# Skewing the two head halves of the output product in a recurrent attention kernel

## The chip, the cores and the metric

The kernel runs on one core of a Trainium2 chip. The core has a matrix engine (TensorE, PE in the profile; its weight loads are shown as PEld), VectorE (DVE), ScalarE (ACT), GpSimd (POOL), and SyncE (SP), which issues most of the DMAs. Each engine works through its own queue of instructions, and the engines wait for each other by semaphores.

The metric is the device time of one execution in microseconds (us); less is better. Where a kernel was run several times, the median is given.

## What is computed

Two sublayers on a sequence of 2048 tokens with 640 features. The first is attention that runs segment by segment: each segment of 32 tokens is put behind 8 memory tokens, and the attention output at those 8 places is the memory of the next segment. So the 64 segments form a chain. The second is a feed-forward layer with a squared ReLU, which has no such chain. Cut to what matters here:

```python
for s in range(n_seg):                                # 64 segments of 32 tokens
    xs = x[:, s * seg_len:(s + 1) * seg_len, :]
    h = jnp.concatenate([mem, xs], axis=1)            # 8 memory rows + 32 tokens
    q = jnp.einsum('btd,dhe->bhte', h, Wq)            # 32 heads of 128
    k = jnp.einsum('btd,dhe->bhte', h, Wk)
    v = jnp.einsum('btd,dhe->bhte', h, Wv)
    scores = jnp.einsum('bhqe,bhke->bhqk', q, k) * scale
    p = _softmax(jnp.where(mask[None, None], scores, -1e9), axis=-1)
    o = jnp.einsum('bhqk,bhke->bhqe', p, v)
    o = jnp.einsum('bhte,hed->btd', o, Wo)            # the output product
    mem = o[:, :M, :]                                 # carried to the next segment
    outs.append(o[:, M:, :])
...
h = x + attention(layernorm(x))
h2 = h + relu(layernorm(h) @ w1 + b1) ** 2 @ w2 + b2
```

## The kernel before, in words

**Strips.** The matrix array is used in four column strips of 32: a matmul with 32 columns of weights is written to rows 32k to 32k+31 of a PSUM tile, where k is the strip, and matmuls of different strips can run side by side. A projection (`proj`, L194) runs over five chunks c of the 640 features; for each chunk it issues four matmuls of 512 columns, one for each strip.

**Steps.** `step(b, sp)` (L368) is one segment; b counts blocks of 128 tokens and sp the four segments in one. It projects q and k (L450 to L470) for 32 rows (8 memory rows and the first 24 tokens of the segment), then v, with the scores (L401, L478), the softmax of the memory rows and their values (L431) put in between. What the memory rows do not need is deferred: the token rows' softmax (L523 to L538) runs on DVE, ACT and POOL beside the output product, and the tokens' values are formed one step later (`token_values`, L336). The last eight tokens of each segment ("tails") depend on no memory of their own segment's chain for their projections, so these are made ahead, for four segments at a time.

**Fill.** Work that can be done at any time is kept in a list `fill` of units; `run(fill, n)` (L249) calls the next n. A unit is one chunk of a tail projection (`tail_units`, L257: four matmuls of 512 columns, ten units for one tensor and block) or one tenth of a tail output product (`wo_tail_units`, L285: one or two rounds of four matmuls of 320 columns). The loop at L715 adds ten units to most steps; some steps get five, a few none. A step calls one unit at L509, two at L520, five at L549 between the output product and `mem_to_hT`, and the rest at L553. The last unit of a projected half evacuates its PSUM tile with ScalarE (`tail_out`, L272).

**The output product and what hangs on it.** `wo_rounds` (L229) sums over 32 heads in 16 rounds. Each round has four matmuls of 320 columns: strips 0 and 1 (`kh` = 0) hold the two halves of the 640 features for one half of the heads, strips 2 and 3 (`kh` = 1) the same for the other half of the heads. `wo_out` (L239) then adds the two head halves: ScalarE copies rows 64 to 127 of the PSUM tile `pw` to `otmp` (L243), and VectorE adds them to rows 0 to 63 (L244) to give `o`. From `o`, `mem_to_hT` (L304) makes the transposed memory rows by 20 small matmuls (L308) and a VectorE cast into `hT4` (L310). The first projection of the next step reads `hT4`.

Two other readers stand near. `token_out` (L351) lets ScalarE write the previous segment's token outputs into `oT`, the tile that the output product reads (L353), and then POOL copies the tails' share (L355); `tails_in` (L312) lets POOL place the tail rows of q and k (L314, L315). `store_main` (L328) has SP store `o`.

**Order and waits.** The program is in manual order: every engine gets its instructions in the order in which this code emits them. The waits between engines are put in by the framework, from the tiles that each instruction reads and writes.

Of the kernel before, what the change touches and what calls it, by code (L numbers as in the profile page):

```python
# [11 lines left out]
F32 = mybir.dt.float32  # L12
# [4 lines left out]
def kernel(  # L17
# [16 lines left out]
    nc = tc.nc  # L34
    _, S, D = A_x.shape
    _, H, E = A_Wq.shape
# [6 lines left out]
    DC = D // 128  # L43
    DH = D // 2
# [23 lines left out]
    s1 = ctx.enter_context(tc.tile_pool(name="s1", bufs=1))  # L68
# [31 lines left out]
    oT = const.tile([128, H, NK], BF16)  # L100
    nc.vector.memset(oT[:], 0.0)
    oTts = [const.tile([128, H, 32], BF16, name="oTt%d" % k) for k in range(2)]
# [3 lines left out]
    def head(p):  # L106

        n, g, j = p // 16, p // 4 % 4, p % 4
        return g * HG + j * 2 + n
# [25 lines left out]
    for ch in range(2):  # L135
        nc.sync.dma_start(out=o0[32 * ch:32 * ch + M, :].rearrange("m (c f) -> m c f", f=64),
                            in_=A_mem0[0].rearrange("m (c t f) -> t m c f", t=2, f=64)[ch])
# [53 lines left out]
            hT4s[b] = hT4  # L191
        return out

    def proj(w, by, lhs, n, ps, c0, c1):  # L194

        if by == "columns":
            wr = w[:].rearrange("p (c g j n k e) -> p c n k g j e", c=DC, g=G, n=2, j=4, k=4)
        elif by == "half":
            wr = w[:].rearrange("p (c k j n e) -> p c n k j e", c=DC, k=G, n=2, j=4)
        else:  # L200
            wr = w[:].rearrange("p (c k n f) -> p c n k f", c=DC, k=G, n=2)
        for c in range(c0, c1):
            for k in range(4):
                nc.tensor.matmul(ps[32 * k:32 * k + 32, :], lhsT=lhs(c), rhs=wr[:, c, n, k], start=(c == 0), stop=(c == DC - 1))  # L204

    def mmtile():
        return mm.tile([128, 512], F32, tag="mm", name="ps")
# [18 lines left out]

    wov2 = wo[:].rearrange("p h (c t f) -> p h t c f", t=2, f=64)

    def wo_rounds(lhs, pw, h0, h1):  # L229

        for h in range(h0, h1):
            for kh in range(2):
                for ch in range(2):
                    j = kh * 2 + ch
                    p = h // 8 * 16 + kh * 8 + h % 8
                    nc.tensor.matmul(pw[32 * j:32 * j + 32, 0:DH], lhsT=lhs(p), rhs=wov2[:, head(p), ch],  # L236
                                     start=(h == 0), stop=(h == 15))

    def wo_out(pw):  # L239
        o = o_ring[0]  # L240
        o_ring.append(o_ring.pop(0))
        tmp = s1.tile([128, DH], F32, tag="tk", name="otmp")
        nc.scalar.copy(out=tmp[0:64], in_=pw[64:128, 0:DH])  # L243
        nc.vector.tensor_tensor(out=o[0:64], in0=pw[0:64, 0:DH], in1=tmp[0:64], op=ALU.add)  # L244
        return o

    fill, late, mid, win = [], [], [], []

    def run(q, n):  # L249
        while n > 0 and q:  # L250
            q.pop(0)()
            n -= 1

    def tail_rows(b, c):
        return hTts[b // 4][:, c, b % 4].rearrange("p k s -> p (k s)")

    def tail_units(b, which):  # L257
        w = {"q": wq, "k": wk, "v": wv}[which]
        lhs = lambda c: tail_rows(b, c)
        st = {}  # L260

        def unit(n, c):
            def f():
                if c == 0:
                    st[n] = mmtile()
                proj(w, "columns" if which != "v" else "order", lhs, n, st[n], c, c + 1)
                if c == DC - 1:
                    tail_out(b, which, n, st[n][:])
            return f
        return [unit(n, c) for n in range(2) for c in range(DC)]  # L270

    def tail_out(b, which, n, ps):  # L272
        row = parked.pop(0) if which == "v" and 0 < b and parked else rowtile()[:]
        evac_row(which, row, ps)
        if which == "v":
            eng = nc.sync if b else nc.scalar
            eng.dma_start(out=vt_d[b, 2 * n:2 * n + 2].rearrange("j r f -> r j f"),
                          in_=row.rearrange("r (j f) -> r j f", j=2))
            return
        if n == 0:  # L280
            tails.setdefault(b, {})[which] = s2.tile([128, H, 32], BF16, tag=which + "Tt", name=which + "Tt")
        dst = tails[b][which]
        late.append(lambda: flip(row, dst, n))

    def wo_tail_units(b):  # L285
        st = {}

        def out():
            o = wo_out(st["ps"])
            dst = o_all[:].rearrange("(b s t) d -> b s t d", s=4, t=SEG)  # L290
            for ch in range(2):
                nc.sync.dma_start(out=dst[b, :, HD:SEG, ch * DH:(ch + 1) * DH], in_=o[32 * ch:32 * ch + 32, :])

        def unit(k):
            def f():
                if k == 0:
                    st["ps"] = mmtile()
                wo_rounds(lambda p: oTts[b % 2][:, p, :], st["ps"], k * 16 // 10, (k + 1) * 16 // 10)
                if k == 9:
                    late.append(out)  # L300
            return f
        return [unit(k) for k in range(10)]

    def mem_to_hT(o, hT4, sp):  # L304
        pm = chn.tile([128, 512], F32, tag="ch", name="pm")
        for c in range(DC):
            for q in range(4):
                nc.tensor.matmul(pm[32 * q:32 * q + 32, c * M:(c + 1) * M], lhsT=o[:, (2 * c + q % 2) * 32:(2 * c + q % 2 + 1) * 32],  # L308
                                 rhs=ident[:, q // 2 * 32:q // 2 * 32 + M], start=True, stop=True)
        nc.vector.tensor_copy(out=hT4[:, :, sp, 0:M], in_=pm[:, 0:DC * M].rearrange("p (c m) -> p c m", m=M))  # L310

    def tails_in(b, sp):  # L312
        q, k = [tails[b][w][:].rearrange("p h (k s) -> p h s k", s=4)[:, :, sp, :] for w in "qk"]
        nc.gpsimd.tensor_copy(out=qT[:, :, SEG:NK], in_=q)  # L314
        nc.gpsimd.tensor_copy(out=kT[:, :, SEG:2 * SEG].rearrange("p h (j k) -> p h j k", k=TL),  # L315
                              in_=k.unsqueeze(2).to_broadcast([128, H, 4, TL]))
# [51 lines left out]
    def step(b, sp, v=None):  # L368
# [3 lines left out]
        lhs = lambda c: hT4[:, c, sp, :]  # L372
        ready = v is not None
        if not ready:
            v = s2.tile([128, EG], BF16, tag="v", name="v")
# [4 lines left out]
        def project(which, w, dst, n, between=None):  # L380
            if ready:
                if between:
                    between()
                return
            ps = mmtile()
            proj(w, "columns", lhs, n, ps, 0, DC)
            row = rowtile()
            if not between:
                evac_row(which, row[:], ps[:])
                flip(row[:], dst, n)  # L390
                return
            for u in range(2):
                nc.scalar.copy(out=row[:, u * 256:(u + 1) * 256], in_=ps[:, u * 256:(u + 1) * 256])  # L393
            between()
            for u in range(2):
                nc.vector.transpose(out=dst[:, n * 16 + u * 8:n * 16 + u * 8 + 8, 0:32],
                                    in_=row[:, u * 256:(u + 1) * 256].rearrange("p (h e) -> p h e", e=32))
# [74 lines left out]
        if not ready:  # L472
            ps0 = mmtile()
            proj(wv, "half", lhs, 0, ps0, 0, 2)
# [49 lines left out]
        tk = s1.tile([128, HG, NK], F32, tag="tk", name="tk")  # L524
# [14 lines left out]
                                op=ALU.mult)  # L539

        pw = chn.tile([128, 512], F32, tag="ch", name="pw")
        wo_rounds(lambda p: oT[:, p, 0:32], pw, 0, 16)
        o = wo_out(pw)
        if s:
            token_out(s - 1, po)
        if s > 1:
            store_main(o, s - 2)
        if not last:
            run(fill, 5)  # L549
            mem_to_hT(o, hT4s[(s + 1) // 4], (s + 1) % 4)  # L550
            tails_in((s + 1) // 4, (s + 1) % 4)
        run(mid, 2)
# [162 lines left out]
    for b in range(NB):  # L715
        for sp in range(4):
# [39 lines left out]
            if 2 <= e <= NK4 + 1:  # L756
                late.append(lambda e=e: prep_stats0(e - 2))
                mid.append(lambda e=e: prep_norm0(e - 2))
            step(b, sp, v0 if b + sp == 0 else None)

    def end_output(s):
        pw = chn.tile([128, 512], F32, tag="ch", name="pw")
        wo_rounds(lambda p: oT[:, p, 0:32], pw, 0, 16)
        store_main(wo_out(pw), s)
# [15 lines left out]
    for t in range(S // NT):  # L780
        hnT = hnTs[t % 2]
        more = t + 1 < S // NT
        got, hts, mvs, hn_ = {}, {}, {}, {}
# [3 lines left out]
        for fc in range(FC):  # L787
            ps = mmtile()
# [8 lines left out]
            w = NT if fc < FFULL else HT  # L797
# [3 lines left out]
            if more and fc >= 1 and (fc - 1) // 3 < NK4:  # L801
                k, stage = divmod(fc - 1, 3)
# [10 lines left out]
        for q in range(NK4):  # L813
# [6 lines left out]
            for hh in range(2):  # L820
                k = pr + 2 * hh
# [3 lines left out]
                if more and q and (hh == 0 or q == 1):  # L825
                    k = q if hh == 0 and q > 1 else hh
# [5 lines left out]
            for hh in range(2):  # L832
                b = t * NK4 + pr + 2 * hh
# [38 lines left out]
```

## Time and profile before

| What | Value |
|---|---|
| Time, median of 3 runs | 1039.55 us (1038.3 to 1039.93) |
| Span of the profiled execution | 1035.5 us |
| TensorE busy in it | 980.1 us (95%) |
| First output product of the chain | at 66.10 us |
| 64 output products (L236 into pw), to | 906 us |
| L236 matmuls into pw | x4224, 159.6 us busy |
| Mean of one matmul of 320 columns | 300 ns |
| Mean of one matmul of 512 columns (L204) | 379 ns |
| Copy L243, mean of one | 422 ns |
| Add L244, mean of one | 482 ns |

The span runs from the first to the last instruction of the profiled execution; the time of a run has some 4 us more around it. A busy time is the union over an engine's instructions: four matmuls of 300 ns that run side by side count little more than one. In the page's groups the columns are line, engine, operation, output and inputs by name, count, then busy time and the mean of one, then the idle time of the engine just before and what ended it. In a timeline a bracket gives the idle time of that engine before the group and the instruction that ended it.

### The profile page before, as it was taken

The numbers are of one execution on the slowest core, as the hardware profiler recorded it, in microseconds if no ns is written. First come the engines' busy times: TensorE is split into PE (matmuls) and PEld (weight loads), VectorE is DVE, ScalarE is ACT, GpSimd is POOL, SyncE is SP. The second block draws the span as 40 slices with busy tenths as digits, with TensorE's granted clock in tenths as the row PEclk, the third lists the DMA queues.
The fourth block names the chain that finished last, engine by engine and source line by source line (L and its number), as shares of the span: only waits on it lengthen the run. The fifth ranks groups of instructions, "written<-read, shape, count | busy, mean of one in ns | idle before, by whom it ended". The sixth has DMA issues, their size and how long they took to land.

```text
span 1035.5 us, 58905 instructions
## 1 busy us (share of the span) xinstructions
PE 980.1 (95%) x26960; PEld 563.9 (54%) x26960; DVE 621.6 (60%) x1740; ACT 536.0 (52%) x1225; POOL 312.3 (30%) x805
## 2 busy tenths in 40 slices
PE   5879899999999999999999999999999998999998
PEld 2335455555655555555555655555555555555565
DVE  2155666766566666666666666666666676565432
ACT  2435555555555555555555555555555555534431
POOL 1033333333333333332333233333333333343210
PEclk9889999999999999999999999999999999999999
DMA  8960101000100000000000000000000110612200
GB/s 319 405 205 26 22 7 31 7 24 6 32 10 22 15 24 24 16 20 14 26 15 22 15 27 15 22 15 27 15 21 8 47 33 7 194 54 72 77 26 26
DMA packets 39112, 51.58 MB, mean 50 GB/s; under 512 B 6160, under 2 KB 34960, under 8 KB 36944
## 3 DMA queue, kind: packets, MB, share of 16 engines
q1 hardware_dynamic: 38000, 47.30, 13.8%
q8 instruction: 210, 3.44, 1.4%
q14 instruction: 38, 0.31, 0.1%
q10 hardware_dynamic: 544, 0.26, 0.1%
q0 software_dynamic: 320, 0.26, 0.1%
HBM read 38.37 MB, written 9.44 MB: 46 GB/s over the span
## 4 chain that ended last, share of the span: by engine, by line
PE 83%; DMA 6%; DVE 5%; issue 3%; ACT 2%; POOL 0%; SPq 0%; DVEq 0%; ACTq 0%; POOLq 0%
PE ps L204 45%; PE pw L236 13%; PE y L823 6%; PE ps L791 5%; PE ps L236 3%; DMA xt<-in_A_x_dram 3%; PE po L437 2%; PE pm L308 2%; PE sm L409 2%; DMA wq<-in_B_w_dram 1%; PE po L343 1%; PE ps L485 1%; ACT em L418 1%; DMA vt_d<-row 1%; DVE o L244 1%
## 5 line engine op out<-in xcount | busy, mean ns | idle before, releaser
L204 PEld LDWEIGHTS <-hT 128*32 128x32 bf16 x7680 | 186.9, 96 | 180.8 <-DVE hT L310 19.6
L204 PE MATMUL ps<-wv,hT 128*32 128x512 bf16 x2520 | 169.9, 379 | 0.7 <-ACT v L492 0.7
L236 PE MATMUL pw<-wo,oT 128*32 128x320 bf16 x4224 | 159.6, 300 | 3.3 <-DVE pTt L555 1.2
L204 PE MATMUL ps<-wq,hT 128*32 128x512 bf16 x2520 | 158.1, 380 | 4.8 <-DVE hT L310 4.8
L204 PE MATMUL ps<-wk,hT 128*32 128x512 bf16 x2520 | 157.6, 379 | 0.0
L236 PEld LDWEIGHTS <-oT 128*32 128x32 bf16 x4224 | 109.3, 97 | 50.7 <-DVE oT L211 15.8
L535 POOL TENSOR_TENSOR pkt<-ek,rk 128x64 bf16<-128x64 bf16 x64 | 18.8, 294 | 377.6 <-DVE rk L533 377.6
L220 ACT ACTIVATE row<-ps 128x512 bf16<-128x512 f32 x156 | 91.9, 601 | 78.4 <-PE ps L204 74.6
L225 DVE STREAM_TRANSPOSE qT<-row 128x512 bf16<-128x512 bf16 x128 | 90.6, 709 | 51.9 <-ACT row L220 51.9
L222 ACT CAST row<-ps 128x512 bf16<-128x512 f32 x115 | 65.9, 596 | 34.3 <-PE ps L204 34.3
L315 POOL COPY kT<-kTt 128x1024 bf16<-128x1024 bf16 x64 | 70.9, 1108 | 13.7 <-DVE kTt L225 13.7
L362 POOL COPY qz<-qT 128x96 bf16<-128x96 bf16 x126 | 33.4, 265 | 125.0 <-DVE qT L225 121.5
L353 ACT CAST oT<-po 128x512 bf16<-128x512 f32 x128 | 68.7, 589 | 1.6
L244 DVE TENSOR_TENSOR o<-pw,otmp 64x320 bf16<-64x320 f32 x66 | 31.8, 482 | 61.9 <-ACT otmp L243 61.9
L204 PEld LDWEIGHTS <-hTt 128*32 128x32 bf16 x1920 | 48.8, 99 | 35.6 <-issue 9.9
L225 DVE STREAM_TRANSPOSE kT<-row 128x512 bf16<-128x512 bf16 x65 | 46.0, 708 | 31.1 <-ACT row L222 31.1
L243 ACT COPY otmp<-pw 64x320 f32<-64x320 f32 x66 | 27.9, 422 | 70.9 <-PE pw L236 70.9
L823 PE MATMUL y<-wq,wk 128*128 128x320 bf16 x416 | 60.9, 299 | 0.0
L393 ACT CAST row<-ps 128x256 bf16<-128x256 f32 x126 | 40.7, 375 | 29.1 <-PE ps L204 29.0
L531 DVE TENSOR_REDUCE zk<-ek 128x8 f32<-128x320 bf16 x64 | 31.1, 486 | 40.2 <-ACT ek L527 40.2
L527 ACT ACTIVATE ek<-tk 128x320 bf16<-128x320 f32 x64 | 30.1, 470 | 45.1 <-DVE tk L525 45.1
L418 ACT ACTIVATE em<-sm,mx 128x64 bf16<-128x64 f32 x126 | 40.4, 321 | 24.3 <-DVE mx L415 24.3
(114 smaller groups left out, 1657.5 us busy)
## 6 DMA issues: line engine op xcount, KB each, us to landing
wv<-in_A_Wv_dram SPq DMA_DIRECT2D x5, 1024.0 KB
wq<-in_A_Wq_dram SPq DMA_DIRECT2D x5, 1024.0 KB
wk<-in_A_Wk_dram SPq DMA_DIRECT2D x5, 1024.0 KB
wo<-in_A_Wo_dram SPq DMA_DIRECT2D x4, 1280.0 KB
vt<-vt_d SPq DMA_DIRECT2D x60, 64.0 KB
xt<-in_A_x_dram SPq DMA_DIRECT2D x20, 160.0 KB
vt_d<-row SPq DMA_DIRECT2D x22, 128.0 KB
wq<-in_B_w_dram SPq DMA_DIRECT2D x1, 2080.0 KB
```

The costliest lines, as they stand in the source:

```text
L204: nc.tensor.matmul(ps[32 * k:32 * k + 32, :], lhsT=lhs(c), rhs=wr[:, c, n, k], start=(c == 0), stop=(c == DC - 1))
L220: nc.scalar.mul(out=row, in_=ps, mul=scale)
L222: nc.scalar.copy(out=row, in_=ps)
L225: nc.vector.transpose(out=dst[:, n * 16:(n + 1) * 16, 0:32], in_=row.rearrange("p (h e) -> p h e", e=32))
L236: nc.tensor.matmul(pw[32 * j:32 * j + 32, 0:DH], lhsT=lhs(p), rhs=wov2[:, head(p), ch], start=(h == 0), stop=(h == 15))
L244: nc.vector.tensor_tensor(out=o[0:64], in0=pw[0:64, 0:DH], in1=tmp[0:64], op=ALU.add)
L315: nc.gpsimd.tensor_copy(out=kT[:, :, SEG:2 * SEG].rearrange("p h (j k) -> p h j k", k=TL), in_=k.unsqueeze(2).to_broadcast([128, H, 4, TL]))
L353: nc.scalar.copy(out=oTg[:, n, :, :, M:NK], in_=po[:, :, n * 128:(n + 1) * 128].rearrange("p g (j q) -> p g j q", q=32))
L393: nc.scalar.copy(out=row[:, u * 256:(u + 1) * 256], in_=ps[:, u * 256:(u + 1) * 256])
L418: nc.scalar.activation(out=em[:], in_=sms[n][:, 0:2 * SEG], func=ACT.Exp, bias=mx[:, 0:1], scale=1.0, accum_out=zm[:])
L791: nc.tensor.matmul(ps[:], lhsT=w1[:, c, fc * 128:(fc + 1) * 128], rhs=hnT[:, c, :], start=(c == 0), stop=(c == DC - 1))
L823: nc.tensor.matmul(y[:, hh, 0:DH], lhsT=f1T[:, fc, k * 128:(k + 1) * 128], rhs=w2[:, fc, cs], start=(fc == 0), stop=False, skip_group_chec ...
```

## The change

The diff lets `proj` and `wo_rounds` issue only some of the strips, and lets each fill unit be called by halves: part 0 issues strips 0 and 1, part 1 strips 2 and 3. The output product of a step is now issued by `wo_skewed`. It takes up to three units off the fill list and sorts all of the work by a planned place, counted in columns of a strip: strips 2 and 3 of the output product start at 0, beside part 0 of the units, which has strips 0 and 1; strips 0 and 1 of the output product start where these end (512 columns a unit); after round 16 of strips 2 and 3 (5120 columns) come the copy `otmp` and part 1 of the units, on strips 2 and 3. The add follows at the end. After it a step calls three units in place of five, ahead of `mem_to_hT`; the rest follow it as before. The output products of the last segments (`end_output`) and of the tails keep their order.

```diff
-    def proj(w, by, lhs, n, ps, c0, c1):
+    def proj(w, by, lhs, n, ps, c0, c1, ks=range(4)):
...
-            for k in range(4):
+            for k in ks:
                 nc.tensor.matmul(ps[32 * k:32 * k + 32, :], lhsT=lhs(c), rhs=wr[:, c, n, k], start=(c == 0), stop=(c == DC - 1))
...
-    def wo_rounds(lhs, pw, h0, h1):
+    def wo_rounds(lhs, pw, h0, h1, khs=range(2)):
 
         for h in range(h0, h1):
-            for kh in range(2):
+            for kh in khs:
                 for ch in range(2):
...
-    def wo_out(pw):
+    def wo_half(pw):
+        tmp = s1.tile([128, DH], F32, tag="tk", name="otmp")
+        nc.scalar.copy(out=tmp[0:64], in_=pw[64:128, 0:DH])
+        return tmp
+
+    def wo_out(pw, tmp=None):
         o = o_ring[0]
         o_ring.append(o_ring.pop(0))
-        tmp = s1.tile([128, DH], F32, tag="tk", name="otmp")
-        nc.scalar.copy(out=tmp[0:64], in_=pw[64:128, 0:DH])
+        if tmp is None:
+            tmp = wo_half(pw)
         nc.vector.tensor_tensor(out=o[0:64], in0=pw[0:64, 0:DH], in1=tmp[0:64], op=ALU.add)
         return o
...
+    def strips(part):
+        return range(4) if part is None else range(2 * part, 2 * part + 2)
+
+    def wo_skewed(lhs, pw, n):
+
+        units = [fill.pop(0) for _ in range(min(n, len(fill)))]
+        lead = 512 * len(units)
+        got, work = [], []
+        for h in range(16):
+            work.append((DH * h, 0, lambda h=h: wo_rounds(lhs, pw, h, h + 1, (1,))))
+            work.append((lead + DH * h, 1, lambda h=h: wo_rounds(lhs, pw, h, h + 1, (0,))))
+        work.append((DH * 16, 2, lambda: got.append(wo_half(pw))))
+        for i, u in enumerate(units):
+            work.append((512 * i, 3, lambda u=u: u(0)))
+            work.append((DH * 16 + 512 * i, 3, lambda u=u: u(1)))
+        for _, _, f in sorted(work, key=lambda w: w[:2]):
+            f()
+        return got[0]
...
         def unit(n, c):
-            def f():
-                if c == 0:
+            def f(part=None):
+                if c == 0 and part != 1:
                     st[n] = mmtile()
-                proj(w, "columns" if which != "v" else "order", lhs, n, st[n], c, c + 1)
-                if c == DC - 1:
+                proj(w, "columns" if which != "v" else "order", lhs, n, st[n], c, c + 1, strips(part))
+                if c == DC - 1 and part != 0:
                     tail_out(b, which, n, st[n][:])
             return f
...
-                wo_rounds(lambda p: oTts[b % 2][:, p, :], st["ps"], k * 16 // 10, (k + 1) * 16 // 10)
-                if k == 9:
+                wo_rounds(lambda p: oTts[b % 2][:, p, :], st["ps"], k * 16 // 10, (k + 1) * 16 // 10,
+                          range(2) if part is None else (part,))
+                if k == 9 and part != 0:
                     late.append(out)
...
         pw = chn.tile([128, 512], F32, tag="ch", name="pw")
-        wo_rounds(lambda p: oT[:, p, 0:32], pw, 0, 16)
-        o = wo_out(pw)
+        half = wo_skewed(lambda p: oT[:, p, 0:32], pw, 3)
+        o = wo_out(pw, half)
         if s:
             token_out(s - 1, po)
         if s > 1:
             store_main(o, s - 2)
         if not last:
-            run(fill, 5)
+            run(fill, 3)
             mem_to_hT(o, hT4s[(s + 1) // 4], (s + 1) % 4)
             tails_in((s + 1) // 4, (s + 1) % 4)
```

More of the change, by code (lines that the diff above doesn't have):

```diff
@@ L294, in unit, with f @@
         def unit(k):
-            def f():
-                if k == 0:
+            def f(part=None):
+                if k == 0 and part != 1:
                     st["ps"] = mmtile()
-                wo_rounds(lambda p: oTts[b % 2][:, p, :], st["ps"], k * 16 // 10, (k + 1) * 16 // 10)
-                if k == 9:
+                wo_rounds(lambda p: oTts[b % 2][:, p, :], st["ps"], k * 16 // 10, (k + 1) * 16 // 10,
+                          range(2) if part is None else (part,))
+                if k == 9 and part != 0:
                     late.append(out)
```

## The prediction

> **What bounds the kernel now.** I read the page first: its span, the engines' busy times, and the engines' shares of the chain that ended last. All times are in us.
>
> ```profile
> span 1035.5 us, 58905 instructions
> PE 980.1 (95%) x26960; PEld 563.9 (54%) x26960; DVE 621.6 (60%) x1740; ACT 536.0 (52%) x1225; POOL 312.3 (30%) x805
> ...
> PE 83%; DMA 6%; DVE 5%; issue 3%; ACT 2%; POOL 0%; SPq 0%; DVEq 0%; ACTq 0%; POOLq 0%
> ```
>
> TensorE (PE) is busy 95% of the span and holds 83% of the chain, so a stop of TensorE lengthens the span unless some later wait gives it back. Second, the timeline of TensorE around one output product (L236), a step with ten fill units; columns are start, duration, engine, line and tiles.
>
> ```profile
> 500.61 2.36 PE L236 MATMUL pw<-wo,oT 128*32 128x320 bf16 x64
> 502.80 1.25 PE L204 MATMUL ps<-wq,hTt 128*32 128x512 bf16 x20
> 503.08 0.42 ACT L243 COPY otmp<-pw 64x320 f32<-64x320 f32 x1 [1.03 <-PE pw L236]
> 503.53 0.48 DVE L244 TENSOR_TENSOR o<-pw,otmp 64x320 bf16<-64x320 f32 x1 [0.73 <-ACT otmp L243]
> 504.07 0.29 PE L308 MATMUL pm<-ident,o 128*32 128x8 bf16 x20
> 504.21 0.60 PE L204 MATMUL ps<-wq,hTt 128*32 128x512 bf16 x8
> 504.45 0.20 DVE L310 CAST hT<-pm 128x40 bf16<-128x40 f32 x1 [0.43 <-PE pm L308]
> 504.70 1.26 PE L204 MATMUL ps<-wq,hT 128*32 128x512 bf16 x20
> 505.79 1.25 PE L204 MATMUL ps<-wk,hT 128*32 128x512 bf16 x20
> ```
>
> Counted from the first pw matmul (500.61): copy at 2.47, add at 2.92, L308 at 3.46, next step's first projection (I call it Q) at 4.09. The 20 fill matmuls of five units cover the copy and the add: there is no bracket on L308, so TensorE shows no wait. The first pw round of four to the first fill round is 2.19 for 16 rounds: 0.137 for a round of four strips of 320 columns. From 504.70 to 505.79, five rounds of 512: 0.217 each. Third, a step with five fill units, and who TensorE waits for.
>
> ```profile
> 329.02 2.37 PE L236 MATMUL pw<-wo,oT 128*32 128x320 bf16 x64
> 331.21 0.60 PE L204 MATMUL ps<-wv,hTt 128*32 128x512 bf16 x8
> ...
> 332.48 0.29 PE L308 MATMUL pm<-ident,o 128*32 128x8 bf16 x20 [0.67 <-DVE o L244]
> 333.12 1.26 PE L204 MATMUL ps<-wq,hT 128*32 128x512 bf16 x20 [0.34 <-DVE hT L310]
> ```
> ```profile
> PE pm L308 <- DVE o L244: 12.3, 14, 1.6
> ...
> PE ps L204 <- DVE hT L310: 4.8, 14, 0.3
> ```
>
> The pause that the change is about exists in 14 steps and costs 12.3 us in all; the other 50 steps have nothing there to win.
>
> **The change part by part.** Which steps: by the loop's fill rules, 7 of the 64 recurrent steps have no unit at the output product, 8 have two left of five (6 projection, 2 tail output), 49 have seven left of ten (35 projection, 14 tail output). With no unit the new order is strips 2, 3, 0, 1 in each round and the copy comes last: nothing changes there.
>
> *The number of instructions* is unchanged, matmuls, copies, adds and DMAs alike. Fill before L308 goes from 5 units to 3 + 3, so after it from 2 to 1.
>
> *A wait is added.* The built order of the changed kernel shows what the diff does not: in 57 steps (49 + 8) a pw matmul of strip 0 waits for ScalarE, namely for the copy otmp; in the kernel before none of L236 does. The rounds of strips 0 and 1 emitted after the copy write the tile that the copy reads, and the two are kept apart by tile, though the copy reads rows 64 to 127 and those matmuls write rows 0 to 63. It stands after 12 of the 16 rounds of strips 0 and 1 (13 with two units). And the copy waits not for the last round of strips 2 and 3 but for the latest pw matmul emitted before it, strip 1 of round 12 (13). Behind the waiting matmul on TensorE's queue stand the last rounds, the second halves of the later units, three whole units and L308; nothing can pass.
>
> *The cost, ten units, projection fill,* from the first pw matmul: strips 0 and 1 run three half units, 3 x 0.217 = 0.65, then round 12 starts at 0.65 + 11 x 0.137 = 2.16. From the start of a last pw round to the copy is 503.08 - (502.80 - 0.137) = 0.42: the copy starts at 2.58, later than the 2.47 of now, and ends 0.42 on, at 3.00. For the way back from ScalarE to TensorE there is no row: add's end to L308 is 504.07 - 504.01 = 0.06, copy's end to add 0.03, pw's end to the copy 0.11; I take 0.06, as it also ends on TensorE (0.03 and 0.11 move the total by -2 and +3). So round 13 starts at 3.06 instead of 2.29, a stop of 0.77, partly beside one half unit on strips 2 and 3. Round 16 starts at 3.06 + 3 x 0.137 = 3.47; to the add 0.40 (L308's end to its reader is 0.09, pw's to the copy 0.11, so 0.02 less than 0.42): 3.87, + 0.48 + 0.06: L308 at 4.41. The three units after pw (0.65, to 4.25) cover most of that. L308 to Q is 504.70 - 504.07 = 0.63 by the DVE cast, which one unit (0.14 + 0.22) cannot stretch: Q at 5.04, against 4.09: +0.95, times 35 = 33.2.
>
> *Tail-output fill:* the three half units are 2, 2 and 1 rounds of 320, so round 12 starts at (5 + 11) x 0.137 = 2.19, and by the same steps Q at 5.07 against 4.12 (as after 316.14): +0.95, times 14 = 13.3. *Two units, projection:* round 13 starts at 0.43 + 12 x 0.137 = 2.08, copy 2.50 to 2.92, three rounds from 2.98, the last at 3.25, add 3.65, L308 4.19, Q 4.82 against 4.10: +0.72, times 6 = 4.3. *Two units, tail output:* round 13 starts at (4 + 12) x 0.137 = 2.19, Q 4.93 against 4.08: +0.85, times 2 = 1.7. Sum +52.5.
>
> *Costed at nothing.* The evacuation of a fill unit now comes ahead of L353 on ScalarE, so the POOL copies of qT and kT end some 0.35 later against Q; kT's copy ended 1.96 after Q (506.66) and its reader L409 comes 4.3 after Q, which hides it; without that cover 0.35 a step, 17 in all. SP's stores follow the add and nothing waits for them in the step.
>
> *Two costs that no row shows.* Strips with matmuls of 320 and 512 columns side by side: now all four strips start within one round. Best, each strip runs on its own (0, taken, as this is how four equal ones run); worst, that I hold possible for the likeliest case, half a round of 320 lost per step, 0.07 x 57 = +4. And TensorE's stops marked "issue": the first pw matmuls at 275.20 and 802.89 are ten groups of four steps apart, 52.8 a group, where the undisturbed steps take 12.85 + 12.85 + 13.17 + 12.88 = 51.75; so about 15 us over 60 steps are lost to late instructions. A stop of 0.8 a step may let them catch up: between 0 and -15. The stops that ended in "issue" lie mostly at L437 to L236, ahead of the new wait, so I take -2. Total +50.5. It is made on the span of 1035.5; the median of the runs, 1039.55, lies 4.05 above it, which I keep: 1090.
>
> **The rivals.** *The wait binds no one* (the copy is done before round 13 or hardly later). The page PSUM — Partial Sum Buffer of the Trainium skill, section on PSUM bank collisions, asks to guard by bank and quadrant, and by it the copy and strips 0 and 1 need no wait, since they are in different quadrants; the built order, with 57 waits, is the guard of a whole tile. Without a wait round 16 starts at 0.65 + 15 x 0.137 = 2.71, add 3.11, L308 3.65, Q 4.28: still +0.19 against 4.09, as L308 now comes after six units and the add, with one unit left to cover the cast. 35 x 0.19 + 14 x 0.19 - 6 x 0.04 + 2 x 0.09 = +9: 1049. For it: only that the rows are disjoint. Against: the waits in the build.
>
> *Strips of unequal length do not overlap four at a time but only in pairs.* Then 32 pairs of 0.137 and six half units of 0.217 take 5.7 instead of 2.84, +2.8 a step on top of the wait, 57 x 2.8 = 160 in all: 1250. Against: at 500.13 eight matmuls of 512 last 0.61 and pw starts at 500.61, both lines overlapping without loss.
>
> *Faster: instructions arrive in time.* The wait is void as in the first rival, and the spread order of L236 removes the whole 15 us of late instructions, +9 - 15 = -6: 1034. It decides once more than 9 comes back. For: the 15 us are real. Against: the number of instructions is the same, and most of these stops come ahead of the product.
>
> *The change does not do what it says* is part of my forecast: the copy is not sooner but 0.1 later.
>
> **How the numbers follow.** The wait decides: 0.90, 1090, its own range 1073 (all 15 back and 0.03 for 0.06) to 1102 (0.11 for 0.06, unequal strips, part of the POOL delay). Void wait 0.05 at 1049; pairs 0.02 at 1250; instructions in time 0.03, at 1034 in 0.02 of it and giving back about what is lost in 0.01. The range 1073 to 1102 leaves out the three rivals and little else. A measurement here tells 0.2%, about 2 us: faster 0.02, same 0.01, slower 0.97.
>
> **What would show it.** After: pw matmuls with an idle time before them ended by ACT otmp, 57 of them, each with strips 0 and 1 empty for about 0.75; the copy some 2.6 after the first pw matmul, L308 at about 4.4, Q near 5.0 in steps of ten units; steps without units unchanged. ACT's copy starting at 2.2 to 2.4, or no stop in pw, would prove the main step wrong; a copy as said but a span near 1050 would mean that later waits give the stop back.

## The result, and the profile after

| | Before | After |
|---|---|---|
| Time, median | 1039.57 us (1038.3 to 1039.93, 4 runs) | 1089.2 us (1088.69 to 1092.97, 4 runs) |
| Span of the profiled execution | 1035.5 us | 1086.9 us |
| First pw matmul of the first to that of the last output product | 827.8 us | 878.1 us |

The changed kernel is slower: 1.0486 times the time before, 95% interval 1.0467 to 1.0504. The difference of the spans is 51.4 us, and 50.3 of it lies between the first and the last output product (66.10 to 893.89 before, 66.97 to 945.06 after, the starts of the first pw matmuls in the timeline). The x4224 matmuls of L236 into pw are 66 products of 64 matmuls: 64 of the chain and the two of `end_output`. So the 906 us in the table of the time before is the end of those two; the last product of the chain starts at 893.89.

First the page of the changed kernel: span, busy times, shares of the chain by engine, and two groups. In a group the number behind the bar is the busy time, then the mean of one, then the idle time just before and what ended it.

```profile
span 1086.9 us, 58951 instructions
...
PE 999.2 (92%) x26951; PEld 588.0 (54%) x26960; DVE 621.6 (57%) x1740; ACT 539.1 (50%) x1225; POOL 309.9 (29%) x805
...
PE 81%; DMA 5%; DVE 5%; ACT 4%; issue 3%; POOL 0%; SPq 0%; ACTq 0%; DVEq 0%; POOLq 0%
...
L236 PE MATMUL pw<-wo,oT 128*32 128x320 bf16 x4224 | 204.8, 300 | 28.0 <-ACT otmp L241 24.6
```

The matmuls are as many as before and one takes as long (300 ns). What is new is the idle time before L236, ended by the copy `otmp` (L241 in this kernel, L243 before), and ScalarE's share of the chain, 4% instead of 2%. The list of TensorE's waits says the same with its number: total, times, longest.

```profile
PE pw L236 <- ACT otmp L241: 24.6, 57, 0.6
PE pm L333 <- DVE o L249: 12.1, 14, 1.6
...
PE ps L204 <- DVE hT L335: 4.7, 14, 0.3
```

57 waits are new; the two old ones, which the change was about, are as they were (12.3 and 4.8 before). The small matmuls are L333 here, the add L249, the cast L335. The timeline of a step with ten projection units shows where the time goes; to be read as the one before the change, from its first pw matmul at 525.51.

```profile
525.51 0.31 PE L236 MATMUL pw<-wo,oT 128*32 128x320 bf16 x2
525.52 0.39 PE L204 MATMUL ps<-wq,hTt 128*32 128x512 bf16 x2
525.66 0.30 PE L236 MATMUL pw<-wo,oT 128*32 128x320 bf16 x2
525.75 0.38 PE L204 MATMUL ps<-wq,hTt 128*32 128x512 bf16 x2
...
526.07 1.91 PE L236 MATMUL pw<-wo,oT 128*32 128x320 bf16 x48
...
527.70 0.38 PE L204 MATMUL ps<-wq,hTt 128*32 128x512 bf16 x2
...
528.08 0.42 ACT L241 COPY otmp<-pw 64x320 f32<-64x320 f32 x1 [1.13 <-PE pw L236]
...
528.55 0.31 PE L236 MATMUL pw<-wo,oT 128*32 128x320 bf16 x2 [0.47 <-ACT otmp L241]
...
529.36 0.48 DVE L249 TENSOR_TENSOR o<-pw,otmp 64x320 bf16<-64x320 f32 x1 [1.66 <-PE pw L236]
...
529.90 0.29 PE L333 MATMUL pm<-ident,o 128*32 128x8 bf16 x20
...
530.53 1.26 PE L204 MATMUL ps<-wq,hT 128*32 128x512 bf16 x20
```

The pairs of pw start every 0.14 and the pairs of the units every 0.22, each on its own strips. The copy starts at 2.57 after the first pw matmul, 0.1 later than before. The next pw pair starts at 3.04, when the copy is over; the bracket shows 0.47 of idle time, because half a unit still runs on strips 2 and 3 (527.70). Strips 0 and 1 stand longer: by the spacing of 0.14 their next pair would have started at about 2.3. The small matmuls come at 4.39 and the next step's first projection at 5.02, against 3.46 and 4.09 before.

### The profile page after: what moved, and what is told of

The parts are those of the page before. It is cut to its first block, busy times and chain, and to the rows that moved or that the text cites. A ratio compares the mean times of both kernels' runs of the same rounds, so it can differ in the third digit from the quotient of the medians.

```text
span 1086.9 us, 58951 instructions
## 1 busy us (share of the span) xinstructions
PE 999.2 (92%) x26951; PEld 588.0 (54%) x26960; DVE 621.6 (57%) x1740; ACT 539.1 (50%) x1225; POOL 309.9 (29%) x805
## 4 chain that ended last, share of the span: by engine, by line
PE 81%; DMA 5%; DVE 5%; ACT 4%; issue 3%; POOL 0%; SPq 0%; ACTq 0%; DVEq 0%; POOLq 0%
PE ps L204 44%; PE pw L236 14%; PE y L848 5%; PE ps L816 4%; DMA xt<-in_A_x_dram 3%; PE ps L236 3%; ACT otmp L241 2%; PE po L462 2%; PE pm L333 2%; PE sm L434 2%; DMA wq<-in_B_w_dram 1%; PE po L368 1%; DVE hT L335 1%; PE ps L510 1%; ACT em L443 1%
## 5 line engine op out<-in xcount | busy, mean ns | idle before, releaser
L236 PE MATMUL pw<-wo,oT 128*32 128x320 bf16 x4224 | 204.8, 300 | 28.0 <-ACT otmp L241 24.6
L236 PEld LDWEIGHTS <-oT 128*32 128x32 bf16 x4224 | 142.4, 97 | 87.3 <-issue 51.1
L249 DVE TENSOR_TENSOR o<-pw,otmp 64x320 bf16<-64x320 f32 x66 | 31.8, 482 | 114.7 <-PE pw L236 104.2
L204 PEld LDWEIGHTS <-hTt 128*32 128x32 bf16 x1920 | 62.7, 98 | 22.2 <-issue 6.2
L241 ACT COPY otmp<-pw 64x320 f32<-64x320 f32 x66 | 27.9, 422 | 77.5 <-PE pw L236 77.5
L236 PE MATMUL ps<-wo,oTt 128*32 128x320 bf16 x1024 | 62.1, 300 | 0.1
L380 POOL COPY oTt<-oT 128x256 bf16<-128x256 bf16 x64 | 26.8, 418 | 118.7 <-ACT oT L378 118.7
L204 PE MATMUL ps<-wk,hTt 128*32 128x512 bf16 x600 | 58.8, 397 | 0.4 <-issue 0.4
L204 PE MATMUL ps<-wq,hTt 128*32 128x512 bf16 x600 | 56.9, 381 | 0.0
```

## The experiments

Times after the first pw matmul are given as in the prediction: copy, L308 (the small matmuls, whatever their line is in a kernel) and Q, the first projection of the next step. An undisturbed step is one with the times that most steps of its kind have.

### The order alone

No unit is skewed in; strips 2 and 3 merely come first in each round.

```diff
-        half = wo_skewed(lambda p: oT[:, p, 0:32], pw, 3)
+        half = wo_skewed(lambda p: oT[:, p, 0:32], pw, 0)
...
-            run(fill, 3)
+            run(fill, 5)
```

> The changed kernel with no fill unit in the skewed product and five units before the small matmuls again: only the order of the strips in a round differs from the kernel before (2, 3, 0, 1). Theory (the price is the wait of strips 0 and 1 for the copy): no such wait, copy at 2.47 us after the first pw matmul, next projection at 4.09, time 1038 to 1042. Rival (putting strips 2 and 3 first costs time by itself): up to the 1089 of the changed kernel.

Measured: 1038.15 us, 1.000 of before (0.9984 to 1.0016). An undisturbed step has its copy at 2.46, L308 at 3.46, Q at 4.09. The order of the strips in a round costs nothing; the rival falls.

### The same skew with one PSUM tile and with two

Both kernels skew two units, in the 35 steps that have seven projection units left, and keep five units ahead of L308. They differ in one thing: in the second, strips 2 and 3 sum into a tile of the pool `mm`, another bank. The skew with three units and two tiles was not run.

```diff
+            f.proj = True
...
-        half = wo_skewed(lambda p: oT[:, p, 0:32], pw, 3)
+        half = None
+        if len(fill) == 7 and hasattr(fill[0], "proj") and not outs:
+            half = wo_skewed(lambda p: oT[:, p, 0:32], pw, 2)
+        else:
+            wo_rounds(lambda p: oT[:, p, 0:32], pw, 0, 16)
...
-            run(fill, 3)
+            run(fill, 5 if half is None else 3)
```

The second kernel has this as well:

```diff
+        hi = mmtile()
...
-            work.append((DH * h, 0, lambda h=h: wo_rounds(lhs, pw, h, h + 1, (1,))))
+            work.append((DH * h, 0, lambda h=h: wo_rounds(lhs, hi, h, h + 1, (1,))))
...
-        work.append((DH * 16, 2, lambda: got.append(wo_half(pw))))
+        work.append((DH * 16, 2, lambda: got.append(wo_half(hi))))
```

> Skew with two units, and only in the 35 steps that have seven projection units left; all other steps as in the kernel before; 2 units + 3 units before the small matmuls, as many as before. Both halves in one PSUM tile as in the change. Theory: 35 waits on the copy, copy at 2.48, small matmuls at 4.17, next projection at 4.8 instead of 4.09: +25, 1064. Rival (the wait costs nothing, the skew does): the same as the version with two tiles.

> The same as the version with two units and one tile, but strips 2 and 3 sum into a PSUM tile of their own (another bank), so that nothing of strips 0 and 1 waits for the copy. Theory: no wait, copy at 2.47, small matmuls at 3.46, next projection at 4.09, time 1038 to 1042, that is, the 25 us come back and nothing is won over the kernel before, since 16 rounds of strips 2 and 3 take 2.19 us wherever strips 0 and 1 are. Rival (unequal lengths side by side, or the skew by itself): 1064 as with one tile. Rival (a free copy is a gain): small matmuls before 3.4, time under 1036.

Measured: one tile 1062.14 us, 1.0236 of before (1.0218 to 1.0253); two tiles 1038.0 us, 0.9997 (0.9983 to 1.001). TensorE's waits with one tile have 35 new ones:

```profile
PE pw L236 <- ACT otmp L241: 13.5, 35, 0.5
```

With two tiles there is none, and the timeline of such a step is (ps is here also the tile of strips 2 and 3):

```profile
355.88 0.31 PE L236 MATMUL ps<-wo,oT 128*32 128x320 bf16 x2
...
358.33 0.42 ACT L241 COPY otmp<-ps 64x320 f32<-64x320 f32 x1 [1.02 <-PE ps L236]
358.37 0.30 PE L236 MATMUL pw<-wo,oT 128*32 128x320 bf16 x2
...
358.81 0.48 DVE L249 TENSOR_TENSOR o<-pw,otmp 64x320 bf16<-64x320 f32 x1 [0.74 <-ACT otmp L241]
...
359.35 0.29 PE L335 MATMUL pm<-ident,o 128*32 128x8 bf16 x20
```

Strips 0 and 1 go on while the copy runs (358.37 beside 358.33). Yet the copy starts at 2.45, the add at 2.93 and L308 at 3.47: the same as in the kernel before. So the whole loss of the skew is the shared tile: 24 us for 35 steps, 0.7 each. And a skew that is free of it wins nothing: strips 2 and 3 still take 16 rounds of 0.137 = 2.19, and the copy starts no earlier. The rival that a free copy is a gain falls too.

### The copy made twice

```diff
-    def wo_half(pw):
+    def wo_half(pw, times=1):
...
-        nc.scalar.copy(out=tmp[0:64], in_=pw[64:128, 0:DH])
+        for _ in range(times):
+            nc.scalar.copy(out=tmp[0:64], in_=pw[64:128, 0:DH])
...
-        work.append((DH * 16, 2, lambda: got.append(wo_half(pw))))
+        work.append((DH * 16, 2, lambda: got.append(wo_half(pw, 2))))
```

> The changed kernel with the copy of a skewed product made twice over, one after the other. Theory (strips 0 and 1 stand until the copy is over, and all that follows is pushed): 57 x 0.42 to 0.46 = +24 to +26, 1113 to 1116, and the stop in pw longer by as much. Rival (the copy is off the path, the order of the matmuls costs): 1089, no change.

Measured: 1125.69 us in two runs (1122.82 and 1128.55), 1.0846 of before (1.0805 to 1.0888). The direction and the mechanism hold, the size was missed.

```profile
PE pw L236 <- ACT otmp L242: 51.0, 57, 1.2
```

The stops in pw grew from 24.6 to 51.0, 0.46 a step, as expected, and L308 moved from 4.38 to 4.84 in an undisturbed step. I had not counted that the six steps with no units run the doubled copy as well (L308 at 3.91 instead of 3.46). That makes 63 x 0.455 = 28.7 of the 34.1 us by which the stretch from the first to the last product is longer than in the changed kernel. The other 5.4 go with TensorE's granted clock: in this stretch of the trace it falls to 0.5 five times, for 3.4 us each (at 114.3, 186.0, 244.0, 592.2 and 824.3), and the changed kernel's trace has 1.0 from 67.1 on. A projection's 20 matmuls took up to 2.19 there, not 1.25. The five steps in which this happens are 9.0 longer than in the changed kernel where 5 x 0.455 = 2.3 was due; the others gave some of that back. All five are steps in which TensorE waits for the add; why the clock falls in them and not in others of that kind is not shown.

### The copy emitted last

The copy comes after all matmuls of the product, and the evacuation of a unit (kept in the list `held` until then) after the copy, so that ScalarE is free for it.

```diff
-        work.append((DH * 16, 2, lambda: got.append(wo_half(pw))))
...
             f()
-        return got[0]
+        half = wo_half(pw)
+        while held:
+            held.pop(0)()
+        holding.clear()
+        return half
...
-                    tail_out(b, which, n, st[n][:])
+                    out = lambda: tail_out(b, which, n, st[n][:])
+                    held.append(out) if holding else out()
```

> The changed kernel, but the copy is emitted after all of the product (and a unit's evacuation after the copy), so that no matmul waits for it; skew, units and their halves as in the change. Theory (what counts is the chain product, copy, add, small matmuls): the stop in pw is gone and pw ends earlier, but copy and add now both stand behind round 16: copy at 3.1 after the first pw matmul, small matmuls at 4.1, next projection at 4.7 against 5.01 in the changed kernel and 4.09 before: 57 x -0.3 = -17 against the change, 1070 to 1075. Rival (the stop of strips 0 and 1 is the whole loss): 57 x 0.75 = 43 come back, 1046 to 1050.

Measured: 1073.82 us in two runs, 1.0327 of before (1.0279 to 1.0374). Copy at 3.11, L308 at 4.10, Q at 4.73. TensorE no longer stops in pw; it waits for the add instead:

```profile
PE pm L340 <- DVE o L249: 37.9, 63, 1.6
```

63 waits where there were 14. The stop is gone and a third of the loss with it, not the whole: what sets Q is the chain of product, copy, add, small matmuls and cast, and this order of it is 0.64 longer than the one before the change.

### Work put under the stop

In the 49 steps of ten units the next three units are called by halves inside the stop. As before, six units come ahead of L308 and one behind it.

```diff
+        more = [fill.pop(0) for _ in range(3)] if len(fill) > 3 else []
         for i, u in enumerate(units):
             work.append((512 * i, 3, lambda u=u: u(0)))
-            work.append((DH * 16 + 512 * i, 3, lambda u=u: u(1)))
+            work.append((DH * 16 + (0 if more else 512 * i), 4 + i, lambda u=u: u(1)))
+        for i, u in enumerate(more):
+            work.append((DH * 16, 3.5 + i, lambda u=u: u(0)))
+            work.append((DH * 16 + 257 + 512 * i, 3, lambda u=u: u(1)))
...
+        covered.append(bool(more))
...
-            run(fill, 3)
+            run(fill, 0 if covered[-1] else 3)
```

> The changed kernel with the next three units put under the stop: their halves for strips 0 and 1 stand between the copy and the waiting round, the halves for strips 2 and 3 beside the last rounds, and no whole unit is left between product and small matmuls (49 steps; six units ahead of the small matmuls and one behind, as in the change). Theory (the chain sets the step, and it is not touched): the stop in pw shrinks to under 0.1, but TensorE then waits 0.7 or so for the add, small matmuls at 4.4, time 1086 to 1092. Rival (the strip time lost in the stop is the price, and filling it wins it back): 49 x 0.65 = 32 less, 1057.

Measured: 1089.08 us in two runs, 1.0473 of before (1.044 to 1.0507), the time of the changed kernel. From its timeline:

```profile
317.18 0.42 ACT L241 COPY otmp<-pw 64x320 f32<-64x320 f32 x1 [1.13 <-PE pw L236]
317.65 0.31 PE L236 MATMUL pw<-wo,oT 128*32 128x320 bf16 x2
...
318.47 0.48 DVE L249 TENSOR_TENSOR o<-pw,otmp 64x320 bf16<-64x320 f32 x1 [1.66 <-PE pw L236]
...
319.01 0.29 PE L340 MATMUL pm<-ident,o 128*32 128x8 bf16 x20 [0.52 <-DVE o L249]
```

The bracket before the waiting pair is gone (317.65), and a bracket of 0.52 stands before L308 (319.01), which comes at the same 4.39 as in the changed kernel (first pw matmul 314.62). The idle time moved, the step did not get shorter. So in these steps it is not strip time that the change loses, but the length of a chain.

### The copy one round earlier in the order

```diff
-        work.append((DH * 16, 2, lambda: got.append(wo_half(pw))))
+        work.append((DH * 15, 2, lambda: got.append(wo_half(pw))))
```

> The changed kernel with the copy emitted straight after round 16 of strips 2 and 3, one round of strips 0 and 1 earlier in TensorE's order. Theory (the copy waits for the latest pw matmul emitted ahead of it, and strips 0 and 1 for the copy): copy at 2.46 to 2.48 instead of 2.56 in steps of ten units, but five rounds instead of four are left behind it, small matmuls at 4.4 to 4.45: 0 to +3, 1088 to 1093. Rival (the copy waits for its own last round or for the end of another matmul): copy at 2.56 as before, and the time up by 57 x 0.14 = 8.

Measured: 1092.42 us in two runs, 1.0505 of before (1.0472 to 1.0538). In an undisturbed step the copy starts at 2.45 and L308 at 4.41. So the copy's start follows the latest pw matmul emitted ahead of it, not only its own half, as the prediction had read from the built order. The waits of pw for the copy are 57 as before, 32.7 in all instead of 24.6.

### A shorter chain

None of the orders above shortens the chain, since its first link is 16 rounds. What can be taken off is a link. From the kernel before: one ScalarE copy takes both halves out of PSUM, rounded to bf16 one by one, and the small matmuls add them, with two identities one above the other (`sel`) as their right side. The sum for the store is made from SBUF later.

```diff
...
-        o = wo_out(pw)
+        ob = s1.tile([128, DH], BF16, tag="tk", name="ob")
+        nc.scalar.copy(out=ob[:], in_=pw[:, 0:DH])
...
-            run(fill, 5)
-            mem_to_hT(o, hT4s[(s + 1) // 4], (s + 1) % 4)
+            run(fill, 3)
+            mem_to_hT(ob, hT4s[(s + 1) // 4], (s + 1) % 4, sel)
+        if s > 1:
+            o = o_ring[0]
+            o_ring.append(o_ring.pop(0))
+            nc.gpsimd.tensor_copy(out=o[0:64], in_=ob[64:128])
+            nc.vector.tensor_tensor(out=o[0:64], in0=ob[0:64], in1=o[0:64], op=ALU.add)
```

> From the kernel before: one ScalarE copy takes all 128 rows of pw out of PSUM as bf16, and the small matmuls add the two halves themselves, with a right side that holds two identities one above the other; the add for the store is made later, from SBUF, on GpSimd and VectorE; three units ahead of the small matmuls, the rest behind. This takes the add off the chain. Theory (the chain of copy, add, small matmuls, cast is what bounds 14 steps and just about bounds the others): small matmuls at 2.46 + 0.47 + 0.06 = 3.0 instead of 3.46, next projection at 3.85 instead of 4.09 in 49 steps (then bound by TensorE's work), and 0.45 less in 14: -12 and -6, 1019 to 1025. Rival (TensorE's work is the bound where units cover the chain): only the 14 steps gain, 1032 to 1034.

Measured: 1048.24 us in four runs, 1.0077 of before (1.0051 to 1.0102): a miss, and on the other side. L308 did come at 2.96 and Q at 3.96 in an undisturbed step with projection units, 0.13 sooner. But a step that had taken 12.85 now often took 13.13 (508.64 to 521.77, say). TensorE's waits have entries that the kernel before has not, or hardly: scores waiting for GpSimd's spread of q (7.9 in all, 0.5 before) and for VectorE's transposes of k.

```profile
PE sm L412 <- POOL qz L365: 7.9, 6, 4.1
...
PE sm L412 <- DVE kT L228: 3.0, 12, 0.3
```

The add for the store stood in VectorE's queue ahead of those transposes, and waited for GpSimd's copy (41.6 in 29 waits). But the largest single wait, 4.1 of the 7.9, has another origin:

```profile
116.25 0.20 POOL L587 CAST b1f<-b1b 128x14 f32<-128x14 bf16 x1 [4.75 <-DMA b1b<-in_B_b_dram]
...
116.71 0.40 PE L412 MATMUL sm<-kT,qz 128*32 128x64 bf16 x16 [4.07 <-POOL qz L365]
```

The spread of q stands in GpSimd's queue behind a cast that waits for a load of `b1b`. SP issues that load behind the stores of `o`; the later add made these later, and the load's last issue moved from 109.75 to 111.41. TensorE's granted clock was 0.5 from 115.1 to 121.9 as well. This one step took 18.97 instead of 13.64, 5.3 of the 10.4 by which the stretch from the first to the last product is longer than before.

So the next version makes the copy for the store on ScalarE, right behind the first one, and calls four units ahead of L308. Against the version above:

```diff
         nc.scalar.copy(out=ob[:], in_=pw[:, 0:DH])
+        if s > 1:
+            o = o_ring[0]
+            o_ring.append(o_ring.pop(0))
+            nc.scalar.copy(out=o[0:64], in_=ob[64:128])
...
-            run(fill, 3)
+            run(fill, 4)
...
-            nc.gpsimd.tensor_copy(out=o[0:64], in_=ob[64:128])
```

> As the version in which one copy takes both halves, but the shifted copy for the store's add is made by ScalarE right behind the first copy instead of by GpSimd, so that VectorE's add for the store, now straight behind the cast, no longer stands in VectorE's queue waiting for GpSimd's copy; four units ahead of the small matmuls. Theory (the late add held up VectorE's transposes of q and k and with them the next scores): small matmuls at 3.0 to 3.1, next projection at 3.85 to 3.95, steps of projection fill 12.6 to 12.7 instead of 13.1, time 1022 to 1030, below the kernel before. Rival (the shorter chain only uncovers the next bound, of ScalarE, VectorE and GpSimd between two steps): 1036 to 1048.

Measured: 1024.08 us (1020.6 to 1029.17, 4 runs), 0.985 of before (0.9827 to 0.9874): 1.5% less, and all four runs lie below all of before. The profile is of the slowest of the four. A step, from its timeline (first pw matmul at 500.27):

```profile
502.45 1.04 PE L207 MATMUL ps<-wq,hTt 128*32 128x512 bf16 x16
...
502.73 0.42 ACT L547 CAST ob<-pw 128x320 bf16<-128x320 f32 x1 [1.03 <-PE pw L239]
503.19 0.46 ACT L551 COPY o<-ob 64x320 bf16<-64x320 bf16 x1
...
503.31 0.28 PE L311 MATMUL pm<-sel,ob 128*32 128x8 bf16 x20
...
503.44 0.82 PE L207 MATMUL ps<-wq,hTt 128*32 128x512 bf16 x12
...
503.70 0.20 DVE L313 CAST hT<-pm 128x40 bf16<-128x40 f32 x1 [1.25 <-PE pm L311]
...
504.09 1.25 PE L207 MATMUL ps<-wq,hT 128*32 128x512 bf16 x20
```

L308 at 3.04 and Q at 3.82, 0.27 sooner than before the change; the next product starts at 512.84, 12.57 after this one. In this stretch TensorE's own work is the bound: 502.45 + 4 x 0.217 = 503.32 for L308, 503.44 + 3 x 0.217 = 504.09 for Q, and both start there.

Before the change they started later than that, although no bracket stood before them: in the prediction's rows 502.80 + 5 x 0.217 = 503.89 and L308 came at 504.07, 504.21 + 2 x 0.217 = 504.64 and Q came at 504.70. A matmul of 512 columns lasts 379 ns in the profile and the next round can start after 217, so a stop of this length is covered by the records of matmuls still running. The weight loads of L308, in the profile before, do name the wait:

```profile
504.07 0.19 PEld L308 LDWEIGHTS <-o 128*32 128x32 bf16 x20 [0.52 <-DVE o L244]
```

So such a step had 0.18 + 0.06 = 0.24 to win, and the shorter chain won 0.27.

The scores' wait for GpSimd's spread is down to one of 2.5, in the step of the `b1b` load, which still takes 16.70 against 13.64 before. Two things were changed at once between the two versions, the engine of the copy and the number of units; that the copy's place was the cause is argued from the waits, not separated.

## Why the prediction was right

It forecast 1090 by one mechanism, and both the time and the mechanism came out; that the time fits to 1 us is in part luck, as the last terms show. Point by point, for undisturbed steps of the profiled execution (Q, and what it moved by):

| Step of the prediction | Forecast | Measured |
|---|---|---|
| Waits of pw for the copy | 57 | 57 |
| Copy, ten units, projection | 2.58 | 2.56 |
| L308, Q | 4.41, 5.04 | 4.38, 5.01 |
| Price, ten units, projection (35 steps) | +0.95 | +0.92 |
| Price, ten units, tail output (14) | +0.95 | +0.89 |
| Price, two units, projection (6) | +0.72 | +0.70 |
| Price, two units, tail output (2, both disturbed) | +0.85 | +1.02 |
| Time lost in a group of four steps, put down to late instructions | back by little | 1.0 before, 0.8 after |
| Change of the whole | +50.5 | +51.4 in the span, 1.0486 in the runs |

- *What bounds.* TensorE's stop lengthened the span, as said: nothing later gave it back. But the forecast's ground, that a stop of a 95% busy engine costs its length, is not quite the reason. With the stop filled the time was the same. What bounds in these steps is the chain from the product to Q, and before the change five units covered all but about 0.2 of it. The working was right because it had followed that chain to Q and not multiplied the stop (0.77 x 57 = 44, or the 24.6 that the profile shows as idle).
- *The wait, and that the diff does not show it.* Right, and shown by the pair with one and two tiles: 24 us for 35 steps with everything else the same.
- *What releases the copy.* Right: the latest pw matmul emitted before it. Moving the copy up by one round moved its start by 0.11.
- *Back from ScalarE to TensorE.* Taken as 0.06 between 0.03 and 0.11; the trace of the change has 528.55 - 528.50 = 0.05.
- *Strips of unequal length.* Taken to run each on its own, and they did: pairs of pw 0.14 apart beside pairs of the units 0.22 apart. The bound of half a round a step was not needed; the rival of pairs falls.
- *A reading that was wrong.* The missing bracket on L308 was taken to mean that 50 steps have nothing to win there. A step of ten units and projection fill had 0.24, as the starts of the rounds show, and the shorter chain won 0.27 there and 0.20 in a step of ten units and tail-output fill. The forecast does not rest on this reading, since it followed the starts and not the brackets.
- *Late instructions.* Ten groups of four steps from 286.63 to 847.77 take 56.11 each. Undisturbed, a group takes 13.78 + 13.78 + 14.10 + 13.79, with 13.56 for one 13.78 where the step has two units: 55.3 on average. So 0.8 is lost a group, where 1.0 was lost before. In the whole stretch the undisturbed steps are 51.4 longer in sum and the stretch is 50.3 longer, so about 1 came back, where 2 had been taken. That late instructions are the cause is not shown: TensorE's waits list only 4.4 us before the change that ended in "issue", of the 15 put down to them.
- *Luck.* The steps were priced 1.1 too high in sum (52.5 for 51.4) and 2 was taken as given back where about 1 was; the two nearly cancel. The span agrees to 1 us (50.5 for 51.4) because 0.9 came in ahead of the first product, where the change does nothing. And the 4.05 between span and median is no constant: the profiled run of the changed kernel took 1088.73 at a span of 1086.9, and the median lies 2.3 above that span.
- *The rivals.* Void wait: the waits were there. Faster by instructions in time: no. That the copy would not be sooner was part of the forecast, and it started 0.1 later.

What the first rival said of a skew with three units and no wait, +9, was not measured; without the wait, with two units, the skew was worth nothing either way.

## What to carry to other kernels

Before work is reordered to let one half of a result be read early, look at how the two halves are kept apart: if both lie in one tile that is guarded as a whole, the reader stops the writer of the other half, and the built order of the changed kernel shows it as a new wait. Put the halves in two banks, or leave the order alone. And ask whether the half gets done sooner at all: strips that already run side by side at their own rate do not finish earlier when they are listed first. Follow the chain from the first to the last link, to the work that waits for it, and price the change by that; idle time that a profile shows is neither the loss nor what filling it would win. A link taken off the chain is worth more than a better order of its links, if what takes its place stays out of the queues that the chain goes through.

## What the runs showed that was not expected

- Filling a stop of TensorE with useful work, in 49 steps, changed the time by nothing (1089.08 against 1089.2 us), though TensorE is busy 92% of the span.
- Half of a loss may not show as idle time of the engine: of 51 us, the profile lists 24.6 as TensorE's waits for the copy, because one strip pair's matmuls count as busy TensorE while the other pair has nothing.
- A stop of 0.18 before the small matmuls had no bracket in the timeline; it shows in the starts of the rounds and in the weight loads.
- A shorter chain made the kernel slower at first (1048.24 us). Half of that is one step, in which a load stood on SP's queue behind the stores that had moved, and the granted clock was 0.5 for 6.8 us. The rest is argued from the waits: the add for the store stood in VectorE's queue ahead of transposes that the next scores wait for.
- Doubling the copy cost 5.4 us more than the chain explains, with five stretches of 3.4 us at a granted clock of 0.5.
- TensorE lost 1.0 us in a group of four steps on top of the undisturbed steps, and still 0.8 when each step had 0.9 us more of slack.
